# Banded attention in front of a mixture of experts: the row maxima leave the exponential, and copies change engines

## The chip, the cores and the metric

The kernel runs on one core of one Trainium2 chip. The metric is device time in microseconds (us) for one execution; smaller is better. Five engines of the core matter here, each with its own queue that is worked off in order: TensorE (PE; its weight loads are shown apart as PEld), VectorE (DVE), ScalarE (ACT), GpSimd (POOL) and SyncE (SP), which only issues DMAs here.

## The reference, cut to what matters

```python
scores = (1 / sqrt(64)) * q @ k.T            # batch 8, heads 8, sequence 576, head size 64
mask   = (rel >= 0) & (rel < 64)             # rel = row position - column position
scores = where(mask, scores, -1e9)
scores = scores - max(scores, axis=-1)       # row maximum
attn   = exp(scores)
attn   = attn / (sum(attn, axis=-1) + 1e-9)
x      = attn @ v                            # 4608 tokens x 512

logits = x @ w_gate                          # 8 experts, 576 tokens each at most
# (token, expert) pairs taken in descending order of logit; each token gets one expert
out[mask_e] = relu(x[mask_e] @ w1[e]) @ w2[e]
```

## The kernel before

**Three stages.** The attention comes first (to about 162 us in the profile), then the first pass of the routing, then the experts with the later routing passes between them. All instructions are put down in an order written by hand; each engine keeps that order, and waits only for the data or buffers of its next instruction. The change touches only the attention and the constants that the routing prepares while the attention runs.

**Attention.** A row block has 64 query rows, and needs the 128 keys that end with its own. Two blocks make 128 partitions; with `m` counting the pairs of blocks (36) and `g` the two halves of the eight heads, there are 72 units `(m, g)`, each of four heads. The loop over `s` (76 iterations) is a software pipeline over these units, and in iteration `s` it puts down:

- `qk` for unit `s`: 16 small score products on PE into `Sp` in PSUM (L126), then on DVE for each of the four heads one custom operation (L135) that adds the mask, scales, writes the negated scores `st`, and leaves the row minimum of them in a column of `mx` (a second, short instruction reads that accumulator). After each of the four, one small step of `norm` for unit `s-4` follows: `r` = row sum + 1e-9 (L203), its reciprocal (L204), the gate values (L188, and every eighth time a sum over heads, L192), the values `x` (L198).
- `sm` for unit `s-1`: four exponentials on ACT, one for each head, with the column of `mx` as bias (L145), giving `pe`.
- `tr` for unit `s-2`: four transposes on PE into the one PSUM buffer `Tp` (L152) and one copy of all four to `pt` on ACT (L154).
- `pv` for unit `s-3`: 16 products on PE with `pt` as weights and the values as moving data (L173). The last of the 73 columns of a value row is 1, so the row sum comes with it; columns 64 to 71 hold the gate products.
- whatever is put down for that iteration in a table `at`, one step of the routing's choices (`late`, six small DVE operations for every four pairs `m`), and one step of the routing's constants (`setup`, a generator; three steps in iterations 4 to 9).

**Values.** `VO[b]` holds a batch's value rows for odd blocks as loaded. `VE[b]` is the same moved by 64 partitions, for even blocks; `even` makes it with two 64x584 copies for each of its four slices `j` (L111, L112), on GpSimd, except the first two slices of batch 0, which are on VectorE. The gate columns are computed on the side, for each batch in two parts: `gate_mm` (PE, L85), `gate_cp` (ACT, L89) in one iteration, `gate_tr` (PE, L95), `gate_out` (DVE, L101 and L104, into columns 64 to 71 of `VO`) and `even` in the next. For batch 2 these iterations are 15 to 18, and then 24 to 27, 34 to 37, 43 to 46, 52 to 55 and 61 to 64. All four gate steps share one PSUM buffer `pvt`.

**Loads.** SP issues the loads of batch `b` in iteration 9(b-2)+5, in the order `VT`, `Q`, `K`, `VO`; a load waits until its buffer is free (two of `VT`, three of the others).

**Constants.** `constants` makes tables for the routing in 64 small steps, 61 of them on DVE (L386 to L437) and three on GpSimd (L401, L403).

Of the kernel before, what the change touches and what calls it, by code (L numbers as in the profile page):

```python
# [30 lines left out]
def attention(ctx, tc, c, q, k, v, vt, gate, xs, L, choices, setup, counters):  # L31
# [65 lines left out]
    def gate_out(b, i0, i1):  # L97
# [16 lines left out]
    PT_, PB, ST, OP_ = {}, {}, {}, {}  # L114

    def qk(m, g, old):
# [13 lines left out]
        st = wk.tile([128, 4, 128], FT, name="st")  # L130
        mx = wk.tile([128, 4], FT, name="mx")
        nrm = norm(*old) if old else []
        for h in range(4):
# [3 lines left out]
            if nrm:  # L137
                nrm.pop(0)()
        ST[m, g] = (st, mx)

    def sm(m, g):
        st, mx = ST.pop((m, g))
        pe = wk.tile([128, 4, 128], FT, name="pe")
        for h in range(4):
            nc.scalar.activation(pe[:, h, :], st[:, h, :], AF.Exp, bias=mx[:, h:h + 1], scale=-1.0)  # L145
        PB[m, g] = pe

    def tr(m, g):
        Tp = ps.tile([128, 4, 128], FT, name="Tp", bufs=1)
        pe = PB.pop((m, g))  # L150
# [26 lines left out]
    def norm(m, g):  # L177
# [52 lines left out]
    for b in range(B):  # L230
        s0 = 9 * (b - 1) + (6 if b < 4 else 7)
        for i, s in zip(PARTS, ((1, 5), (7, 11))[b] if b < 2 else (s0, s0 + 2)):
# [13 lines left out]

    for s in range(n + 4):
        old = seq[s - 4] if 4 <= s else None
        if s < n:
            qk(*seq[s], old)  # L250
        else:
            rs, inv, gates, values = norm(*old)

            for f in (rs, inv, values, gates) if s < n + 2 else (rs, inv, gates):
                f()
# [15 lines left out]
        if late:  # L271
            late.pop(0)()
        if s > 3:
            for _ in range(3 if s < 10 else 1):
# [794 lines left out]
```

## Time and profile before

| | us |
|---|---|
| median of 3 runs | 668.48 (667.67 to 670.57) |
| the profiled execution | 668.27 |
| its span, first to last instruction | 666.6 |
| PE busy | 634.8 (95%) |
| DVE busy | 444.3 (67%) |
| ACT busy | 363.2 (54%) |
| POOL busy | 187.8 (28%) |

The span is 1.67 us shorter than the execution's own time. Busy shares are averages over three stages with different limits; PE's end times are modelled, so a PE that is shown busy may be waiting for short times, and the distances between starts are the safer reading. In a row of the timeline the columns are the start in us, the duration in us, engine, line, operation, output<-input, shapes, count of merged instructions, and in square brackets how long the engine had been idle and what ended that.

### The profile page before, as it was taken

To read this page: it belongs to the slowest core of one execution; us is meant where nothing else is said; L and a number is where in the kernel's file an instruction comes from. 1 tells how busy PE (TensorE), PEld (TensorE's weight loads), DVE (VectorE), ACT (ScalarE), POOL (GpSimd) and SP (SyncE) were. 2 spreads that over 40 slices of the span, in tenths; PEclk is the share of its full clock that TensorE was granted. 3 is DMA by queue.
4 is the path that set the end of the run, shared out by engine and by line. 5 is a ranking of instruction groups with operands and counts; after the bars stand their busy time and mean duration, and the time that the engine had idled before them with its cause. 6 is when DMAs were issued, how large, how long until landed. Compare 5 with 4: busy or idle time off the path is not lost. (4 is left out here: it accounts for less than half of the span.)

```text
span 666.6 us, 16956 instructions
## 1 busy us (share of the span) xinstructions
PE 634.8 (95%) x6383; PEld 533.4 (80%) x6383; DVE 444.3 (67%) x2246; ACT 363.2 (54%) x734; POOL 187.8 (28%) x218
## 2 busy tenths in 40 slices
PE   7989999998579999999999999999999999999995
PEld 5667777776459878987997898789789879988984
DVE  5878898888777766885786688478668852303300
ACT  5778998886046247427624652762465276256310
POOL 0433233330052034206202420620252062042211
PEclk8999999999579999999999999999999999999999
DMA  9999988922068369829766982976698299939701
GB/s 302 342 370 372 372 324 311 390 79 74 10 205 212 67 215 237 182 58 289 200 118 228 220 191 58 287 196 117 228 212 186 60 294 270 234 99 222 143 25 47
DMA packets 50097, 134.10 MB, mean 201 GB/s; under 512 B 4696, under 2 KB 10968, under 8 KB 50016
## 3 DMA queue, kind: packets, MB, share of 16 engines
q0 software_dynamic: 15280, 52.98, 35.7%
q1 hardware_dynamic: 34192, 79.52, 33.4%
q8 instruction: 50, 0.82, 0.5%
q10 hardware_dynamic: 544, 0.52, 0.2%
q14 instruction: 31, 0.25, 0.1%
HBM read 82.15 MB, written 18.87 MB: 152 GB/s over the span
## 5 line engine op out<-in xcount | busy, mean ns | idle before, releaser
L949 POOL DMA_INDIRECT out<-ot,idx x40 | 41.6, 1041 | 299.2 <-DVE ab L629 100.9
L899 ACT ACTIVATE hh<-h 128x256 fp32r<-128x256 f32 (+1 forms) x128 | 52.2, 408 | 105.5 <-PE h L927 104.5
L969 PE MATMUL o<-wh,hl 128*128 128x512 f32 x256 | 102.8, 401 | 0.0
L969 PE MATMUL o<-wl,hh 128*128 128x512 f32 x256 | 101.8, 397 | 0.0
L969 PE MATMUL o<-wh,hh 128*128 128x512 f32 x256 | 101.5, 397 | 0.0
L927 PE MATMUL h<-xh,wl 128*128 128x256 f32 (+1 forms) x512 | 93.2, 299 | 0.0
L135 DVE CUSTOM_DVE_ANT_0 st<-Sp,mask 128x128 f32<-128x128 f32 x288 | 78.9, 278 | 20.8 <-PE Sp L126 14.1
L145 ACT ACTIVATE pe<-st,mx 128x128 f32<-128x128 f32 x288 | 91.2, 391 | 2.7 <-DVE mx L135 2.7
L927 PE MATMUL h<-xl,wh 128*128 128x256 f32 (+1 forms) x512 | 92.0, 298 | 0.4 <-DVE xl L860 0.4
L927 PE MATMUL h<-xh,wh 128*128 128x256 f32 (+1 forms) x512 | 90.9, 299 | 0.7 <-ACT xh L856 0.7
L904 DVE SCALAR_TENSOR_TENSOR hl<-h,hh 128x256 fp32r<-128x256 f32 x128 | 53.4, 417 | 56.7 <-ACT hh L899 55.7
L927 PEld LDWEIGHTS h<-xh,wh 128*128 128x128 f32 x512 | 75.5, 189 | 1.6 <-ACT xh L856 0.8
L927 PEld LDWEIGHTS h<-xh,wl 128*128 128x128 f32 x512 | 76.2, 189 | 0.2
L927 PEld LDWEIGHTS h<-xl,wh 128*128 128x128 f32 x512 | 75.5, 189 | 0.7 <-DVE xl L860 0.6
L811 ACT ACTIVATE wh<-st 128x1024 fp32r<-128x1024 f32 x64 | 67.2, 1050 | 6.7 <-DMA st<-w 6.7
L820 ACT ACTIVATE wl<-wh 128x1024 fp32r<-128x1024 f32 x61 | 64.4, 1056 | 0.9
L822 POOL DMA_DIRECT2D wl<-st x61 | 57.2, 1258 | 16.0 <-ACT wl L820 15.6
L969 PEld LDWEIGHTS o<-wl,hh 128*128 128x128 f32 x256 | 48.1, 188 | 9.0
L969 PEld LDWEIGHTS o<-wh,hl 128*128 128x128 f32 x256 | 48.3, 189 | 8.7
L969 PEld LDWEIGHTS o<-wh,hh 128*128 128x128 f32 x256 | 48.2, 188 | 8.5
L173 PE MATMUL Op<-VO,pt 128*64 128x73 f32 x640 | 52.4, 233 | 0.4 <-DVE x L198 0.3
L860 DVE TENSOR_TENSOR xl<-tp,xh 128x512 fp32r<-128x512 f32 (+1 forms) x40 | 25.3, 631 | 40.0 <-ACT xh L856 39.9
(178 smaller groups left out, 1117.0 us busy)
## 6 DMA issues: line engine op xcount, KB each, us to landing
wl<-st POOLq DMA_DIRECT2D x61, 512.0 KB
st<-w SPq DMA_DIRECT2D x60, 512.0 KB, 5.7
xs<-x SPq DMA_DIRECT2D x36, 256.0 KB, 5.3
VO<-v SPq DMA_DIRECT2D x6, 1168.0 KB
VT<-vt SPq DMA_DIRECT2D x6, 1152.0 KB, 8.9
Q<-q SPq DMA_DIRECT2D x6, 1152.0 KB
K<-k SPq DMA_DIRECT2D x6, 1152.0 KB, 16.4
VO<-v SPq DMA_DIRECT2D x4, 584.0 KB
```

Source lines behind the costliest of these rows:

```text
L135: nc.vector.tensor_tensor_reduce(st[:, h, :], Sp[h % 2][:, h // 2], mk, scale=-0.125, scalar=3.0e38, op0=OP.add, op1=OP.min, accum_out=mx[ ...
L145: nc.scalar.activation(pe[:, h, :], st[:, h, :], AF.Exp, bias=mx[:, h:h + 1], scale=-1.0)
L173: nc.tensor.matmul(Op[64 * a:64 * a + 64, h, :], pt[:, h, 64 * a:64 * a + 64], vv[a][:, 4 * g + h, :], start=True, stop=True)
L811: nc.scalar.activation(hi, st[i], AF.Copy)
L820: nc.scalar.activation(lo, hi.bitcast(FT), AF.Copy, scale=-1.0)
L822: nc.gpsimd.dma_start(lo.bitcast(FT), st[i], accum_op=OP.add)
L860: nc.vector.tensor_tensor(xl[:, :, r], t[:, :, :n], xh[:, :, r].bitcast(FT), OP.subtract)
L899: nc.scalar.activation(hh[:, f, c0:c1], h, AF.Relu)
L904: nc.vector.scalar_tensor_tensor(t, h[:, a - c0:b - c0], 0.0, hh[:, f, a:b].bitcast(FT), op0=OP.max, op1=OP.subtract)
L927: nc.tensor.matmul(h, wv[:, cc, 128 * (f % 2):128 * (f % 2) + 128], xt[:, cc, c0:c1], start=(k == 0), stop=(k == 11))
L949: nc.gpsimd.indirect_dma_start(out=self.out, out_offset=IndirectOffsetOnAxis(ap=idx[0:m, a:a + 1], axis=0), in_=ot[0:m], in_offset=None)
L969: nc.tensor.matmul(o, ht[:, f, 128 * a:128 * a + 128], wt[:, 512 * (f % 2):512 * (f % 2) + 512], start=(k == 0), stop=(k == 23))
```

## The change

- **Maxima.** `sm` becomes one GpSimd subtraction for all four heads, in place: `st` minus `mx`, the column spread over 128 elements. The transposes take `st`, and the copy after them becomes the exponential of all four heads at once. `st` and `mx` get four buffers instead of three.
- **Row sums.** `r` = sum + 1e-9 goes from DVE to ACT, and is put down at the head of iteration `s`, ahead of everything else of ACT.
- **Gate columns and even blocks.** `gate_out` goes from DVE to ACT. The even blocks go from GpSimd to ACT, but for the first two slices of batch 0, which stay on VectorE; slices 2 and 3 come two and four iterations later than before.
- **Order on VectorE.** Within `qk` the reciprocal and the gate values come after the second head, the values, the step of the choices and the steps of the constants after the third, and the fourth head is last.
- **Constants.** The shift table is made by one operation instead of eight, `gt` by one instead of five, `s5` by two instead of 32, with three more iotas on GpSimd at the start. 23 steps remain.

```diff
@@ gate_out, even
-        nc.vector.tensor_copy(VO[b][:, j0:j1, :, 64:72],
-                              pt[:, :128 * n].rearrange("p (j h g) -> p j h g", j=n, h=8)[:, :, :, :8])
+        nc.scalar.activation(VO[b][:, j0:j1, :, 64:72],
+                             pt[:, :128 * n].rearrange("p (j h g) -> p j h g", j=n, h=8)[:, :, :, :8], AF.Copy)
         if i1 % 2:
-            nc.vector.tensor_copy(VO[b][0:64, 4, :, 64:72],
-                                  pt[:64, 128 * n:128 * n + 128].rearrange("p (h g) -> p h g", h=8)[:, :, :8])
+            nc.scalar.activation(VO[b][0:64, 4, :, 64:72],
+                                 pt[:64, 128 * n:128 * n + 128].rearrange("p (h g) -> p h g", h=8)[:, :, :8], AF.Copy)
...
-    def even(b, j, eng):
-
-        eng.tensor_copy(VE[b][0:64, j], VO[b][64:128, j])
-        eng.tensor_copy(VE[b][64:128, j], VO[b][0:64, j + 1])
+    def even(b, j, early):
+
+        for d, e in ((slice(0, 64), j), (slice(64, 128), j + 1)):
+            a = VE[b][d, j], VO[b][64 - d.start:128 - d.start, e]
+            if early:
+                nc.vector.tensor_copy(*a)
+            else:
+                nc.scalar.activation(*a, AF.Copy)
@@ qk, sm, tr
-        st = wk.tile([128, 4, 128], FT, name="st")
-        mx = wk.tile([128, 4], FT, name="mx")
-        nrm = norm(*old) if old else []
+        st = wk.tile([128, 4, 128], FT, name="st", bufs=4)
+        mx = wk.tile([128, 4], FT, name="mx", bufs=4)
         for h in range(4):
 
             nc.vector.tensor_tensor_reduce(st[:, h, :], Sp[h % 2][:, h // 2], mk, scale=-0.125, scalar=3.0e38,
                                            op0=OP.add, op1=OP.min, accum_out=mx[:, h:h + 1])
-            if nrm:
-                nrm.pop(0)()
+            for f in (nrm[0:2], nrm[2:] + [small])[h - 1] if h in (1, 2) else ():
+                f()
...
-        st, mx = ST.pop((m, g))
-        pe = wk.tile([128, 4, 128], FT, name="pe")
-        for h in range(4):
-            nc.scalar.activation(pe[:, h, :], st[:, h, :], AF.Exp, bias=mx[:, h:h + 1], scale=-1.0)
-        PB[m, g] = pe
+        st, mx = ST[m, g]
+        nc.gpsimd.tensor_tensor(st, st, mx[:, :, None].to_broadcast([128, 4, 128]), OP.subtract)
...
-            nc.tensor.transpose(Tp[:, h, :], pe[:, h, :], c["ident"])
+            nc.tensor.transpose(Tp[:, h, :], st[:, h, :], c["ident"])
         pt = wk.tile([128, 4, 128], FT, name="pt")
-        nc.scalar.activation(pt, Tp, AF.Copy)
+        nc.scalar.activation(pt, Tp, AF.Exp, scale=-1.0)
@@ norm
-        return [lambda: nc.vector.tensor_scalar(r, Op[:, :, 72], 1e-9, None, op0=OP.add),
-                lambda: nc.vector.reciprocal(r, r), gates, values]
+        nc.scalar.activation(r, Op[:, :, 72], AF.Copy, bias=1e-9)
+        return [lambda: nc.vector.reciprocal(r, r), gates, values]
@@ the table at, and the loop over s
-                    put(s + 1, even, b, j, nc.gpsimd if b or j > 1 else nc.vector)
+                    put(s + 1 + 2 * max(0, j - 1), even, b, j, not b and j < 2)
...
+    def small(s):
+        if late:
+            late.pop(0)()
+        if s > 3:
+            for _ in range(3 if s < 10 else 1):
+                next(setup, None)
...
-            qk(*seq[s], old)
+            qk(*seq[s], norm(*old) if old else [], lambda: small(s))
         else:
-            rs, inv, gates, values = norm(*old)
-
-            for f in (rs, inv, values, gates) if s < n + 2 else (rs, inv, gates):
+            inv, gates, values = norm(*old)
+
+            for f in (inv, values, gates) if s < n + 2 else (inv, gates):
@@ constants (counters makes sh and v5 with three iotas)
-        for r in range(NR):
-            yield nc.vector.tensor_scalar(tab[:, r], dg, 28 - 4 * r, None, op0=OP.logical_shift_left)
+        yield nc.vector.tensor_tensor(tab, dg[:, None, :].to_broadcast([128, NR, ND]),
+                                      self.sh[:, :, None].to_broadcast([128, NR, ND]), OP.logical_shift_left)
...
-        for k in range(5):
-
-            yield nc.vector.tensor_scalar(gt[:, k:k + 1], jp[0:32, 8 * k:8 * k + 1], 0.0, None, op0=OP.is_le)
+        yield nc.vector.tensor_scalar(gt, jp[0:32, 0:33:8], 0.0, None, op0=OP.is_le)
...
+        w5 = t("w5", [72, 2, 4, 5])
+        yield nc.vector.tensor_scalar(w5, self.v5, 0.0, None, op0=OP.is_equal)
+        yield nc.vector.scalar_tensor_tensor(s5, self.v5, -36.0, w5, op0=OP.is_equal, op1=OP.add)
```

## Rows read from the trace of the kernel before

**Rows 1.** The page's busy time by engine, and the granted clock and DMA share in 40 slices of 16.7 us.
```profile
PE 634.8 (95%) x6383; PEld 533.4 (80%) x6383; DVE 444.3 (67%) x2246; ACT 363.2 (54%) x734; POOL 187.8 (28%) x218
...
PEclk8999999999579999999999999999999999999999
DMA  9999988922068369829766982976698299939701
```

**Rows 2.** The view of stretches, from iteration 18 to the last score product: length, then busy time and count of PE, PEld, DVE, ACT, POOL, the granted clock, DMA share, GB/s.
```profile
47.20:156.80 109.60, 109.18 (x2024) 80.05 (x2020) 95.68 (x749) 96.57 (x277) 31.61 (x48) 1.00 0.82 296
```

**Rows 3.** The timeline of PEld over one iteration without gate work (31): score products, transposes, the first value product, the next score products.
```profile
78.11 0.43 PEld L126 LDWEIGHTS Sp<-K,Q 64*64 64x64 f32 x16
78.71 0.42 PEld L152 LDWEIGHTS Tp<-ident,pe 128*128 128x128 f32 x4 [0.17 <-ACT pe L145]
79.30 0.13 PEld L173 LDWEIGHTS Op<-VO,pt 128*64 128x64 f32 x1 [0.17 <-DVE mx L135]
...
79.96 0.42 PEld L126 LDWEIGHTS Sp<-K,Q 64*64 64x64 f32 x16
```

**Rows 4.** The timeline of DVE over the same iteration: first and third head, the steps between them, the end, and the next iteration's first head.
```profile
78.94 0.29 DVE L135 CUSTOM_DVE_ANT_0 st<-Sp,mask 128x128 f32<-128x128 f32 x1 [0.18 <-PE Sp L126]
79.16 0.08 DVE L135 DVE_READ_ACCUMULATOR2_ANT mx<- 128x1 f32 x1
79.16 0.16 DVE L203 TENSOR_SCALAR r<-Op 128x4 f32<-128x4 f32 x1
79.23 0.28 DVE L135 CUSTOM_DVE_ANT_0 st<-Sp,mask 128x128 f32<-128x128 f32 x1
...
80.02 0.42 DVE L198 TENSOR_TENSOR x<-Op,r 128x256 f32<-128x256 f32 x1
80.36 0.15 DVE L426 TENSOR_SCALAR sx<-jp 72x4 f32<-72x4 int32 x1
80.79 0.29 DVE L135 CUSTOM_DVE_ANT_0 st<-Sp,mask 128x128 f32<-128x128 f32 x1 [0.28 <-PE Sp L126]
```

**Rows 5.** The groups of instructions by line and shape from 40 to 160 us, ACT and DVE: busy us, mean ns.
```profile
L145 ACT ACTIVATE pe<-st,mx 128x128 f32<-128x128 f32 x228 | 72.2, 391 | 0.0
...
L154 ACT ACTIVATE pt<-Tp 128x512 f32<-128x512 f32 x58 | 34.4, 593 | 6.7 <-PE Tp L152 3.8
...
L89 ACT ACTIVATE vs<-pvt 128x256 f32<-128x256 f32 x6 | 2.3, 384 | 3.6 <-PE pvt L85 3.6
```

**Rows 6.** The page's groups: a long copy on ACT.
```profile
L820 ACT ACTIVATE wl<-wh 128x1024 fp32r<-128x1024 f32 x61 | 64.4, 1056 | 0.9
```

**Rows 7.** The groups by line and shape of POOL up to 160 us.
```profile
L112 POOL COPY VE<-VO 64x584 f32<-64x584 f32 x30 | 20.3, 676 | 19.3 <-DVE VO L101 14.4 <-DVE VO L104 3.8
...
L401 POOL IOTA r<- 128x1152 bf16 x1 | 1.2, 1243 | 0.1
```

**Rows 8.** The timeline of ACT, a copy and the four exponentials behind it.
```profile
79.47 0.60 ACT L154 ACTIVATE pt<-Tp 128x512 f32<-128x512 f32 x1
79.96 1.27 ACT L145 ACTIVATE pe<-st,mx 128x128 f32<-128x128 f32 x4
```

**Rows 9.** The timeline of PEld around the gate work of batch 3 (iterations 27 to 30): transposes of the gate values, then score products and transposes.
```profile
68.25 0.28 PEld L95 LDWEIGHTS pvt<-ident,vs 128*128 128x128 f32 x3
68.73 0.42 PEld L126 LDWEIGHTS Sp<-K,Q 64*64 64x64 f32 x16 [0.20 <-issue]
69.33 0.42 PEld L152 LDWEIGHTS Tp<-ident,pe 128*128 128x128 f32 x4 [0.17 <-ACT pe L145]
...
71.17 0.42 PEld L152 LDWEIGHTS Tp<-ident,pe 128*128 128x128 f32 x4 [0.17 <-ACT pe L145]
...
73.17 0.42 PEld L152 LDWEIGHTS Tp<-ident,pe 128*128 128x128 f32 x4 [0.17 <-ACT pe L145]
```

**Rows 10.** The timeline of DVE and of PE about 46 us (batch 2's gate values, iterations 16 to 18), in this order: one row of DVE, three of PE.
```profile
46.23 0.29 DVE L101 COPY VO<-pvt 128x128 f32<-128x128 f32 x1 [2.96 <-DMA VO<-v]
...
46.57 0.74 PE L85 MATMUL pvt<-VT,wgs 128*32 128x320 f32 x8 [1.50 <-DVE VO L101]
...
47.84 0.66 PE L152 MATMUL Tp<-ident,pe 128*128 128x128 f32 x4
48.84 0.28 PE L173 MATMUL Op<-VO,pt 128*64 128x73 f32 x1 [0.34 <-DVE x L198]
```

**Rows 11.** The waits of PE up to 50 us, summed: what waited for what, us in total, times, longest.
```profile
PE Op L173 <- DVE VE L112: 1.1, 1, 1.1
```

**Rows 12.** The waits from 40 to 160 us: PE's weight loads for GpSimd.
```profile
PEld Op L173 <- POOL VE L112: 0.6, 3, 0.3
```

**Rows 13.** The timeline of DVE: the same comparison of the choices twice.
```profile
37.06 0.43 DVE L449 TENSOR_TENSOR oh<-L,m 128x32 bf16<-128x32 f32 x1
...
73.30 0.17 DVE L449 TENSOR_TENSOR oh<-L,m 128x32 bf16<-128x32 f32 x1
```

**Rows 14.** The timeline of POOL at the first of these.
```profile
36.78 0.67 POOL L112 COPY VE<-VO 64x584 f32<-64x584 f32 x1
```

**Rows 15.** The timeline at the end of the attention: on DVE the first head of the last score products, on PE the last transposes, on ACT the copy behind them, and on DVE the last row sum, its reciprocal, and the last step of the choices.
```profile
157.58 0.29 DVE L135 CUSTOM_DVE_ANT_0 st<-Sp,mask 128x128 f32<-128x128 f32 x1 [0.25 <-PE Sp L126]
...
160.43 0.66 PE L152 MATMUL Tp<-ident,pe 128*128 128x128 f32 x4 [0.36 <-ACT pt L154]
...
161.19 0.60 ACT L154 ACTIVATE pt<-Tp 128x512 f32<-128x512 f32 x1 [0.81 <-PE Tp L152]
...
162.62 0.16 DVE L203 TENSOR_SCALAR r<-Op 128x4 f32<-128x4 f32 x1 [0.21 <-PE Op L173]
162.81 0.18 DVE L204 RECIPROCAL r<-r 128x4 f32<-128x4 f32 x1
...
164.58 0.19 DVE L455 TENSOR_TENSOR one<-w,best 128x32 bf16<-128x32 bf16 x1
```

More of the change, by code (lines that the diff above doesn't have):

```diff
@@ L100, in gate_out, with qk @@
         n = j1 - j0
-        nc.vector.tensor_copy(VO[b][:, j0:j1, :, 64:72],
-                              pt[:, :128 * n].rearrange("p (j h g) -> p j h g", j=n, h=8)[:, :, :, :8])
+        nc.scalar.activation(VO[b][:, j0:j1, :, 64:72],
+                             pt[:, :128 * n].rearrange("p (j h g) -> p j h g", j=n, h=8)[:, :, :, :8], AF.Copy)
         if i1 % 2:
-            nc.vector.tensor_copy(VO[b][0:64, 4, :, 64:72],
-                                  pt[:64, 128 * n:128 * n + 128].rearrange("p (h g) -> p h g", h=8)[:, :, :8])
+            nc.scalar.activation(VO[b][0:64, 4, :, 64:72],
+                                 pt[:64, 128 * n:128 * n + 128].rearrange("p (h g) -> p h g", h=8)[:, :, :8], AF.Copy)
         if not i0:
             VE[b] = ld.tile([128, 4, H, VW], FT, name="VE")
-    def even(b, j, eng):
-        eng.tensor_copy(VE[b][0:64, j], VO[b][64:128, j])
-        eng.tensor_copy(VE[b][64:128, j], VO[b][0:64, j + 1])
-    PT_, PB, ST, OP_ = {}, {}, {}, {}
-    def qk(m, g, old):
+    def even(b, j, early):
[5 more added lines that the diff above has]
+                nc.scalar.activation(*a, AF.Copy)
+    PT_, ST, OP_ = {}, {}, {}
+    def qk(m, g, nrm, small):
         Sp = [t[g] for t in SP]
@@ L136, in qk @@
                                            op0=OP.add, op1=OP.min, accum_out=mx[:, h:h + 1])
-            if nrm:
-                nrm.pop(0)()
+            for f in (nrm[0:2], nrm[2:] + [small])[h - 1] if h in (1, 2) else ():
+                f()
         ST[m, g] = (st, mx)
     def sm(m, g):
-        st, mx = ST.pop((m, g))
-        pe = wk.tile([128, 4, 128], FT, name="pe")
-        for h in range(4):
-            nc.scalar.activation(pe[:, h, :], st[:, h, :], AF.Exp, bias=mx[:, h:h + 1], scale=-1.0)
-        PB[m, g] = pe
+        st, mx = ST[m, g]
+        nc.gpsimd.tensor_tensor(st, st, mx[:, :, None].to_broadcast([128, 4, 128]), OP.subtract)
     def tr(m, g):
         Tp = ps.tile([128, 4, 128], FT, name="Tp", bufs=1)
-        pe = PB.pop((m, g))
+        st, mx = ST.pop((m, g))
         for h in range(4):
-            nc.tensor.transpose(Tp[:, h, :], pe[:, h, :], c["ident"])
+            nc.tensor.transpose(Tp[:, h, :], st[:, h, :], c["ident"])
         pt = wk.tile([128, 4, 128], FT, name="pt")
-        nc.scalar.activation(pt, Tp, AF.Copy)
+        nc.scalar.activation(pt, Tp, AF.Exp, scale=-1.0)
         PT_[m, g] = pt
@@ L270, in attention @@
             f(*a)
-        if late:
+        if s >= n and late:
             late.pop(0)()
-        if s > 3:
-            for _ in range(3 if s < 10 else 1):
-                next(setup, None)
     for f in last:
@@ L368, in __init__ @@
         t("dg", [128, ND], I32)
+        t("sh", [128, NR], I32)
+        t("v5", [72, 2, 4, 5], I32)
         t("lane", [128, 1])
@@ L377, in counters @@
         iota(self.dg, pattern=[[1, ND]], base=1, channel_multiplier=0)
+        iota(self.sh, pattern=[[-4, NR]], base=28, channel_multiplier=0)
+        iota(self.v5, pattern=[[1, 2], [2, 4], [8, 5]], base=0, channel_multiplier=-1)
+        iota(self.v5[:, :, 2:4, 4], pattern=[[1, 2], [2, 2]], base=32, channel_multiplier=-1)
         iota(self.rows, pattern=[[0, 1]], base=0, channel_multiplier=1)
@@ L418, in constants @@
         s5 = t("s5", [72, 2, 4, 5], BF)
-        for h in range(2):
-            for g in range(4):
-                for k in range(2):
-                    n = 5 if g < 2 else 4
-                    o = 36 * k + 2 * g + h
-                    w = t(f"sx{k}", [72, 5])
-                    yield nc.vector.tensor_scalar(w[:, 0:n], jp[0:72, o:o + 8 * n - 7:8], 0.0, None, op0=OP.is_equal)
-                    if g > 1:
-                        yield nc.vector.tensor_scalar(w[:, 4:5], jp[0:72, o + 28:o + 29], 0.0, None, op0=OP.is_equal)
-                    if k:
-                        yield nc.vector.tensor_tensor(s5[:, h, g], w0, w, OP.add)
-                    w0 = w
+        w5 = t("w5", [72, 2, 4, 5])
+        yield nc.vector.tensor_scalar(w5, self.v5, 0.0, None, op0=OP.is_equal)
+        yield nc.vector.scalar_tensor_tensor(s5, self.v5, -36.0, w5, op0=OP.is_equal, op1=OP.add)
         t("st", [128, 5, E])
```

## The prediction

> **What bounds the kernel now.** I read the page first: PE is busy for 95% of the span, and no other engine comes near [rows 1]. That is an average over stages, so I cut the attention out with the view of stretches. From 47.2 us, where iteration 18 begins, to the last score product at 156.8 us, PE is busy 109.18 of 109.60 us, at a granted clock of 1.00 (the 2.4 GHz level), while DVE and ACT both stand at about 88% and POOL at 29% [rows 2]. "Busy" is modelled, so I checked it on the starts of one iteration without gate work: score products at 78.11, transposes at 78.71, value products at 79.30, next score products at 79.96, hence 0.60 + 0.59 + 0.66 = 1.85 us [rows 3]. The 0.17 us ahead of the transposes and of the value products is there with any releaser, so it belongs to PE's own work. DVE waits for PE once in each iteration (0.28 us at 80.79) [rows 4]. So in this stretch the three busy engines are near each other, but PE sets the pace, and the change takes nothing from PE: 16 score products, four transposes and 16 value products stay.
>
> Ahead of the stretch something else rules. At 46.23 DVE's copy of the gate columns of batch 2 had waited 2.96 us for the load of VO, and PE had stood 1.50 us behind it [rows 10]; the DMA engines are at 8 or 9 tenths in every slice up to 83 us [rows 1]. That load is last of three batches in a queue that is always full, and the change moves no load. Whatever the first 46 us gain is lost in this wait, and what they lose is hidden up to the same amount.
>
> **The change part by part.**
>
> *Work taken off DVE and ACT after 47 us: nothing gained.* DVE loses the row sum (0.07 us between starts, 79.16 to 79.23) [rows 4], the gate copies and 41 constant steps; ACT loses four exponentials of 0.391 us for one larger one. PE hides all of it. What can be won is what PE still lost: 109.60 − 109.18 = 0.42 us [rows 2], and of the waits for GpSimd's even blocks three times 0.6/3 − 0.17 = 0.03 us, 0.1 us in all [rows 3, 12]. I take 0.1.
>
> *The subtraction on GpSimd.* No row shows POOL with two inputs. The nearest is its copy of 584 columns, 0.676 us, that is 1.16 ns a column [rows 7]. Bounds for 512 columns: as fast as one input 0.59; three passes (two reads, one write) 1.78. Two inputs read one after the other give 1.19, and I take 1.2. The Trainium skill (GPSIMD Engine Reference, "Performance versus the Vector engine") measures 4497 ns for an addition of 2048 columns and advises against elementwise work there; a quarter is an estimated 1.12 us, which would leave the sum as it is; no run here shows it yet.
>
> Is it in time? Now the fourth head comes last. Counting from DVE's first head: values start at 80.02 − 78.94 = 1.08; without the row sum (0.07) and the fourth head (79.23 − 78.94 less 0.07, 0.22) 0.79; values 0.34 (80.36 − 80.02); a step of the choices up to 0.17 [rows 13]; fourth head 0.22 and its accumulator read 0.08: 1.60. DVE's first head is 0.83 behind PE's score products (78.94 − 78.11), a hand-over costs 0.10 (161.19 less 160.43 + 0.66) [rows 15], so the subtraction runs from 2.53 to 3.73 and PE may go on at 3.83. The transposes of that unit are due at 2 x 1.85 + 0.60 = 4.30. 0.47 us are left: up to 1.67 us the subtraction costs nothing. At 1.78 it would cost 0.1 in each iteration. Behind it on POOL stand only three iotas of the constants (1.24 us the longest [rows 7]), in iterations 6 and 7, ahead of 46 us.
>
> *Gate columns and even blocks on ACT.* ACT takes 0.384 for 256 columns [rows 5] and 1.056 for 1024 [rows 6]: 0.875 ns a column and 0.16 fixed; so 0.67 for an even copy, 0.27 and 0.22 for the two gate copies, 0.16 for a row sum, 0.391 + 384 x 0.875 ns = 0.73 for the new exponential. Two in a row overlap by 0.11 (79.47 + 0.60 against 79.96) [rows 8]. The queue of ACT in an iteration is now: row sum, exponential, gate copies, even copies. The tight place is the second gate iteration of a batch, followed by an iteration without gate work. In batch 3 the gate transposes start at 68.25 and end about 0.51 later (0.66 for four, less one of 0.15) [rows 9, 15]; gate copies from 68.86 (hand-over 0.10) to 69.24, even copies 69.24 to 70.47, row sum to 70.52, exponential 70.41 to 71.14. Behind this exponential waits the next set of transposes, since there is one Tp: released at 71.24, it started at 71.17 before [rows 9]. That is 0.07 late. The row sum at 70.52 holds DVE's reciprocal, and by it the rest of that iteration: 0.1 hand-over, reciprocal and gate values 0.2, third head 0.22, values 0.34, choices 0.17, fourth head 0.30 give 71.85; the subtraction ends at 73.15, and its transposes, at 73.17 before [rows 9], come at 73.25: no later than PE already is. Waits of ACT on its own writes aren't in any row; I take 0.15 a batch. Bounds: 0 (a little idle was there) and 0.7 (no overlap, 4 x 0.11, and two hand-overs more, with the subtraction late behind it). Batches 2 to 7: 6 x 0.15 = 0.9.
>
> *The wait at 46 us moves to ACT.* Behind the gate copy that waits for VO now stand two even copies, a row sum and the exponential: 46.23 + 0.27, + 2 x 0.67 − 0.11, row sum, exponential end at 48.40; Tp is free at 48.50 instead of 47.84, the value products come at 49.10 instead of 48.84 [rows 10]: 0.26.
>
> *Up to 46 us.* PE loses 1.1 us there for even copies on DVE [rows 11], and 1.50 in the wait: 2.6 us of cover. New costs: those two DVE copies beside a subtraction, 0.5 to 1.9; iteration 8, which has two slices for ACT (4 x 0.56, gate copy and exponential 0.8, against an iteration of 2.2), 0.9; iterations 10 and 12, 0.1 to 0.3. 1.5 to 3.1 against 2.6: I take 0, at the worst 0.5. Without that cover it would be the whole sum.
>
> *The end.* The last unit has no successor to hide behind. Its first head was at 157.58; + 1.60 + 0.10 + 1.2 + 0.10 = 160.58 for transposes that stood at 160.43 [rows 15]: 0.15. The exponential is 0.13 longer than the copy; the last row sum goes by ACT, one hand-over more, 0.1. Together 0.4, all in front of the last step of the choices at 164.58, on which the routing waits.
>
> Sum: −0.1 + 0.9 + 0.26 + 0 + 0.4 = 1.5 us. Against the profiled execution (span 666.6 and 1.67 around it, 668.27) that is 669.8; the median of the runs, 668.48, stands 0.2 above that execution, which I leave out. Routing and experts do the same work and only start later.
>
> **The rivals.** *GpSimd's port decides (slower).* A comparison of the choices took 0.43 us instead of 0.17, and ended with the GpSimd copy that ran beside it (37.49 and 37.45) [rows 13, 14]. Four of the six steps of the choices read two SBUF tensors like this one. They now stand between the third and the fourth head, while the subtraction of the unit before may still run, and the next subtraction waits for the fourth head: a loop of subtraction + 0.10 + 0.17 + 0.30. At 1.2 that is 1.77, under 1.85; it decides from 1.28 on. At 1.78 it is 2.35, 0.50 too much in four iterations of eight, seven such groups after 47 us: 14 us, 682. For it: DVE is at 88%. Against: in most iterations the step comes 1.14 + 0.25 us behind the last fourth head, when a subtraction of 1.2 is over.
> The Trainium skill has this rule (SBUF — State Buffer, "SBUF: two separate sides"): DVE operations with two SBUF inputs or in a two-port mode and GpSimd exclude each other for whole instructions; the trace agrees, with the 0.43 above.
>
> *ACT's queue costs more (slower).* At the upper bound, 6 x 0.7 + 0.7 at 46 us + 0.4 = 5.3 us: 673.6. For it: ACT carries 1.12 us of even copies in front of the next exponential. Against: five of nine iterations have no even copies at all, and there they stand behind the exponential.
>
> *PE's last losses go (faster).* If ACT's queue is always in time, the gain is at most 0.42 us [rows 2] and the 0.36 idle at 160.43 [rows 15]: 667.5. That is also the case in which the change does what it says and nobody waits for it.
>
> **How the numbers follow.** About 0.5% (3.3 us) is what a measurement of this kernel can tell from no change: 665.0 to 671.6. My sum (668.5 to 671.6) 0.48; PE's last losses go 0.17; ACT's queue, 671.6 to 674, 0.18; GpSimd's port, 674 to 682, 0.12; something that I don't see and that gains over 3.3 us, 0.05, since a gain after 46 us has no place on PE. So faster 0.05, same 0.65, slower 0.30. The range from 667.0 to 677 leaves out the 0.05, a little of the small gain, and the larger half of the port's case.
>
> **What would show it.** The subtraction's mean near 1.2 us; starts of the score products still 1.85 apart without gate work; PE again waiting for the gate copy (now ACT) at 46.2; after each second gate iteration a transposition that waits for ACT by some tenths; DVE's idle time grown, for PE; the last step of the choices near 166. The prediction is wrong if PE's starts after 47 us are further apart in iterations without gate work (the port), or if VO of batch 2 lands earlier.

## The result, and the profile after

The changed kernel took 673.82 us (median of 5 runs, 671.36 to 674.58); the kernel before, beside it, 668.0. The ratio is 1.0072 (95% interval 1.0053 to 1.009): slower by about 5 us (the ratio is that of the means; the medians are 5.8 us apart). The profiled execution took 673.82 us, with a span of 672.2.

The page's busy time by engine, of the kernel after:
```profile
PE 636.1 (95%) x6383; PEld 533.8 (79%) x6383; DVE 439.1 (65%) x2109; ACT 334.0 (50%) x602; POOL 221.4 (33%) x233
```
The view of stretches, kernel after, from iteration 18 to the last score products (columns as in [rows 2]):
```profile
48.20:162.30 114.10, 110.12 (x2022) 79.96 (x2018) 90.64 (x634) 76.91 (x183) 55.06 (x53) 1.00 0.78 282
```
ACT and DVE got lighter, and GpSimd, which took work over, still has room: ACT is busy for 76.91 us here and for 96.57 before, DVE for 90.64 and 95.68 [rows 2]. Yet the stretch is 4.5 us longer (0.77 of it is a pause of this one execution, experiment 11), and PE, which did the same work, is now idle for 114.10 − 110.12 = 3.98 us of it, against 0.42. Less work on ACT, and PE waits: shares of busy time can't show that, the waits can.

The view of waits, kernel after, 47 to 165 us (us in total, times, longest):
```profile
DVE r L204 <- ACT r L203: 12.4, 20, 1.9
...
PEld Tp L152 <- POOL st L146: 3.0, 9, 0.6
PEld Op L173 <- DVE x L198: 2.5, 8, 0.7
PE Tp L152 <- ACT r L203: 1.8, 7, 0.5
PE Op L173 <- DVE x L198: 1.0, 3, 0.4
```
The first row isn't on PE and would cost nothing by itself. It is the root of the third and fifth, as "The row sum" below shows. The fourth names the row sum, which was the last thing to end; by the code the exponential ahead of it holds `Tp`.

Where PE lost it is read best from the starts of the score products, iteration by iteration. (Counted from the start, the iteration at 78.11 in [rows 3], called 31 there, is 33 when the first is 0, as everywhere else; nothing hangs on it.) A "step to 21", or a loss "at 21", is the distance from the start of iteration 20 to that of 21, so the wait lies in iteration 20. I compare a second execution of each kernel (the runs `before_again` and `after_again` below):

| stretch (iterations) | PE's loss, us | what it waits for |
|---|---|---|
| 0 to 10 | 0.45 | 0.36 at 8, for two even copies on DVE (0.14 against the first profile of before) |
| 11 to 17 | 1.92 | ACT: two slices of even blocks in iteration 8, then one at a time |
| 18 | −1.57 | the wait for VO, which absorbs this |
| 19 to 22 | 1.14 | 0.14 at 19: ACT, two slices in iteration 16; 0.75 at 21: exponential late 0.26, row sum late 0.49; 0.24 at 22: subtraction late |
| 23 to 33 | 0.23 | ACT, batch 3 (the kernel before itself loses 0.14 at 30) |
| 34 to 51 | 0.70 | ACT, batches 4 and 5 |
| 52 to 60 | 0.74 | 0.38 at 53: row sum late; 0.36 at 58 and 59: ACT |
| 61 to 70 | 0.95 | 0.26 at 67: ACT; 0.31 at 69: row sum late; 0.13 at 62 and 0.24 at 70: subtraction late |
| behind them, to the last step of the choices | 0.19 | last unit |

The sum is 4.75 us: the last step of the choices stands at 169.79 instead of 165.04. What follows differs by 1.1 to 1.4 us between two executions of one kernel (502.02 and 503.46 us for the kernel before, 501.87 and 503.01 after), so the 4.3 us between the two spans agree with it.

**A batch, seen on ACT.** ACT, kernel after, second gate iteration of batch 4 and what follows:
```profile
92.74 0.29 ACT L101 ACTIVATE VO<-pvt 128x128 f32<-128x128 f32 x1 [0.55 <-PE pvt L95]
92.92 0.21 ACT L104 ACTIVATE VO<-pvt 64x64 f32<-64x64 f32 x1
93.14 1.40 ACT L116 ACTIVATE VE<-VO 64x584 f32<-64x584 f32 x2
94.57 0.17 ACT L203 ACTIVATE r<-Op 128x4 f32<-128x4 f32 x1
94.64 0.59 ACT L154 ACTIVATE pt<-Tp 128x512 f32<-128x512 f32 x1
```
PEld at the same time:
```profile
94.48 0.43 PEld L130 LDWEIGHTS Sp<-K,Q 64*64 64x64 f32 x16
95.34 0.42 PEld L152 LDWEIGHTS Tp<-ident,st 128*128 128x128 f32 x4 [0.44 <-issue]
...
96.59 0.42 PEld L130 LDWEIGHTS Sp<-K,Q 64*64 64x64 f32 x16
97.29 0.42 PEld L152 LDWEIGHTS Tp<-ident,st 128*128 128x128 f32 x4 [0.27 <-POOL st L146]
```
From the gate copy to the end of the exponential ACT needs 95.23 − 92.74 = 2.49 us. The transposes were due 0.60 behind the score products, at 95.08, and come at 95.34: 0.26 late. One iteration on they are due at 97.19 and come at 97.29, now behind the subtraction: 0.10 more. Together 0.36 in this batch.

**The double slice.** ACT, kernel after, iterations 8 and 9:
```profile
26.63 1.39 ACT L116 ACTIVATE VE<-VO 64x584 f32<-64x584 f32 x2
28.05 0.29 ACT L101 ACTIVATE VO<-pvt 128x128 f32<-128x128 f32 x1
28.37 1.39 ACT L116 ACTIVATE VE<-VO 64x584 f32<-64x584 f32 x2
29.78 0.17 ACT L203 ACTIVATE r<-Op 128x4 f32<-128x4 f32 x1
29.85 0.59 ACT L154 ACTIVATE pt<-Tp 128x512 f32<-128x512 f32 x1
```
PE, the transposes behind that exponential:
```profile
30.59 0.63 PE L152 MATMUL Tp<-ident,st 128*128 128x128 f32 x4 [1.18 <-ACT r L203]
```
**The row sum.** DVE, kernel after, while PE is in iteration 20 (reciprocal, gate values, sum over heads, then values):
```profile
53.31 0.18 DVE L204 RECIPROCAL r<-r 128x4 f32<-128x4 f32 x1 [0.80 <-ACT r L203]
53.52 0.19 DVE L188 TENSOR_TENSOR l<-Op,r 128x32 f32<-128x32 f32 x1
53.75 0.62 DVE L192 TENSOR_REDUCE L<-l 128x32 f32<-128x256 f32 x1
...
54.49 0.42 DVE L198 TENSOR_TENSOR x<-Op,r 128x256 f32<-128x256 f32 x1
```
PEld at the same time, the transposes and the first value product, which needs the buffer `Op` that the values free:
```profile
53.88 0.42 PEld L152 LDWEIGHTS Tp<-ident,st 128*128 128x128 f32 x4 [0.43 <-issue]
54.96 0.13 PEld L173 LDWEIGHTS Op<-VO,pt 128*64 128x64 f32 x1 [0.67 <-DVE x L198]
```
The row sum stood behind two even copies on ACT. DVE had waited 0.80 us for it, every eighth unit sums over heads too (0.62 us), and the values came so late that PE stood. The step from iteration 20 to 21 is 2.61 us after, 1.86 before. With the 0.17 that is always there taken off, 0.26 of the difference is the late exponential, as in batch 4, and about 0.5 the late values.

**A third way.** In iterations that sum over heads, the third and fourth head now stand behind that sum, and so the subtraction does. PEld, kernel after, two iterations on:
```profile
141.50 0.42 PEld L152 LDWEIGHTS Tp<-ident,st 128*128 128x128 f32 x4 [0.30 <-POOL st L146]
```
0.17 of this is there with any releaser [rows 3]; 0.13 is a loss. It returns at 62 in every kernel here with the new order on DVE, and at 70 in all but run 3 below. At 22 and 70 the changed kernel loses 0.24, where the row sum is late as well; with single copies (run 2 below) it is 0.15 and 0.12.

### The profile page after: what moved, and what is told of

The parts are those of the page before. It is cut to its first block, busy times and chain, and to the rows that moved or that the text cites. A ratio compares the mean times of both kernels' runs of the same rounds, so it can differ in the third digit from the quotient of the medians.

```text
span 672.2 us, 16833 instructions
## 1 busy us (share of the span) xinstructions
PE 636.1 (95%) x6383; PEld 533.8 (79%) x6383; DVE 439.1 (65%) x2109; ACT 334.0 (50%) x602; POOL 221.4 (33%) x233
## 5 line engine op out<-in xcount | busy, mean ns | idle before, releaser
L146 POOL TENSOR_TENSOR st<-st,mx 128x512 f32<-128x512 f32 x72 | 75.1, 1042 | 86.2 <-DVE mx L138 70.4
L138 DVE CUSTOM_DVE_ANT_0 st<-Sp,mask 128x128 f32<-128x128 f32 x288 | 73.9, 286 | 17.2 <-PE Sp L130 16.3
L154 ACT ACTIVATE pt<-Tp 128x512 f32<-128x512 f32 x72 | 42.9, 596 | 39.0 <-PE Tp L152 39.0
L965 PEld LDWEIGHTS o<-wh,hh 128*128 128x128 f32 x256 | 48.2, 188 | 8.6
```

Source lines behind the costliest of these rows:

```text
L138: nc.vector.tensor_tensor_reduce(st[:, h, :], Sp[h % 2][:, h // 2], mk, scale=-0.125, scalar=3.0e38, op0=OP.add, op1=OP.min, accum_out=mx[ ...
L146: nc.gpsimd.tensor_tensor(st, st, mx[:, :, None].to_broadcast([128, 4, 128]), OP.subtract)
L154: nc.scalar.activation(pt, Tp, AF.Exp, scale=-1.0)
L965: nc.tensor.matmul(o, ht[:, f, 128 * a:128 * a + 128], wt[:, 512 * (f % 2):512 * (f % 2) + 512], start=(k == 0), stop=(k == 23))
```

## The experiments

Theory: TensorE loses its time to ScalarE's queue, where two even copies of 0.69 us in a row stand in front of a row sum and an exponential. Rivals: the row sum by itself; GpSimd's subtraction or its port; something of the execution and not of the change. Iterations are counted as in the table; run 3 is experiment 3, and so on.

**1. `rsum_dve`: the row sum back on DVE.**
```diff
-        nc.scalar.activation(r, Op[:, :, 72], AF.Copy, bias=1e-9)
-        return [lambda: nc.vector.reciprocal(r, r), gates, values]
+        def inv():
+            nc.vector.tensor_scalar(r, Op[:, :, 72], 1e-9, None, op0=OP.add)
+            nc.vector.reciprocal(r, r)
+        return [inv, gates, values]
```


> Theory: the changed kernel (673.8 us, +5.8 against before) loses its time where ACT's two even copies (1.39 us together) stand in front of the next row sum and the next exponential. DVE waits for row sums for 12.4 us after 47 us, and by that the values and the release of the two Op buffers come late; where the sum over heads (0.62 us) falls into the same iteration, PE waits (0.76 us in iteration 20, 0.38 in 52, 0.54 in 68 and 69). With the row sum back on DVE these three places go, the 0.25 us per batch of the late exponential stay: 671.5 to 672.5 us, and no wait of DVE for a row sum. Rival 1, only the exponential's delay matters: the same three places stay, 673.5 or more. Rival 2, GpSimd's subtraction or its port is what is late: no change, 673.8.

Measured: 672.15 us, 1.0055 (1.0039 to 1.0072). As expected: the step at 21 falls from +0.75 to +0.19, which is the exponential's, the one at 53 from +0.38 to +0.07, and the late exponentials stay. The row sum is a part of the loss, about 1.7 us by the medians, not all of it. The two intervals overlap, so it is the steps that show it: from iteration 18 to the last this profile loses 1.2 us less than that of `after_again`, 1.8 without its pause of 0.63 at 33 (see 11).

**2. `even_split`: the two copies of a slice in successive iterations.**
```diff
-    def even(b, j, early):
...
-        for d, e in ((slice(0, 64), j), (slice(64, 128), j + 1)):
+    def even(b, j, early, part=(0, 1)):
...
+        for d, e in [((slice(0, 64), j), (slice(64, 128), j + 1))[i] for i in part]:
...
-                    put(s + 1 + 2 * max(0, j - 1), even, b, j, not b and j < 2)
+                    if not b and j < 2:
+                        put(s + 1, even, b, j, True)
+                        continue
+                    for k_ in range(2):
+                        put(s + 1 + k_ + 2 * max(0, j - 1) - (not b), even, b, j, False, (k_,))
```
The last slices of batch 0 also come one iteration earlier.

> The same even copies on ACT, but the two of a slice in two successive iterations (one copy an iteration; those of batch 0 one iteration earlier). Theory (the two copies in one go hold up row sum and exponential): the chain in front of them is 0.70 us shorter, so the 0.35 us a batch, the losses at the sums over heads and most of the double slices in iterations 8 and 16 go: 669 to 670.5 us, with PE's starts of score products 1.85 us apart in nearly all iterations without gate work. Rival 1, ACT's total load or a count of its instructions matters: 673 to 674. Rival 2, the subtraction or the port of GpSimd: 673.8.

Measured: 668.58 us, 1.0005 (0.9992 to 1.0017): level with the kernel before, better than expected. ACT, the same place in batch 4:
```profile
90.40 0.29 ACT L101 ACTIVATE VO<-pvt 128x128 f32<-128x128 f32 x1 [0.55 <-PE pvt L95]
90.58 0.21 ACT L104 ACTIVATE VO<-pvt 64x64 f32<-64x64 f32 x1
90.80 0.69 ACT L116 ACTIVATE VE<-VO 64x584 f32<-64x584 f32 x1
91.39 0.15 ACT L203 ACTIVATE r<-Op 128x4 f32<-128x4 f32 x1
91.58 0.60 ACT L154 ACTIVATE pt<-Tp 128x512 f32<-128x512 f32 x1
92.21 0.69 ACT L116 ACTIVATE VE<-VO 64x584 f32<-64x584 f32 x1
```
The view of waits, 47 to 165 us:
```profile
DVE r L204 <- ACT r L203: 2.9, 4, 1.6
...
PEld Op L173 <- DVE x L198: 0.7, 4, 0.2
```
The same work on the same engine, with one copy behind the exponential instead of two in front of it. The steps at 11, 21, 40, 49, 53, 58 and 67 are gone, most of the wait for the row sum with them; 0.15 at 22, 0.13 at 62 and 0.12 at 70 stay.

**3. `even_pool`: the even blocks back on GpSimd at the times of before, all else as changed.**
```diff
-    def even(b, j, early):
...
-                nc.scalar.activation(*a, AF.Copy)
+    def even(b, j, eng):
...
+        eng.tensor_copy(VE[b][0:64, j], VO[b][64:128, j])
+        eng.tensor_copy(VE[b][64:128, j], VO[b][0:64, j + 1])
...
-                    put(s + 1 + 2 * max(0, j - 1), even, b, j, not b and j < 2)
+                    put(s + 1, even, b, j, nc.gpsimd if b or j > 1 else nc.vector)
```


> The even copies back on GpSimd in the iterations of before, all else as changed. Theory: ACT is free, so the losses at ACT go (minus 3 to 4 us), but two copies of 0.67 us stand in front of a subtraction of 1.04 in four of nine iterations, 2.4 against 1.85 us, which uses up the 0.6 us of slack and gives back 0.2 to 0.5 us a batch: 670.5 to 673. If the subtraction and GpSimd's port were what is late in the changed kernel (rival), more work there makes it worse: 675 to 680.

Measured: 695.57 us, 1.0412 (1.039 to 1.0433): a miss, all theories far too low. POOL in the second gate iteration of a batch:
```profile
98.53 1.04 POOL L142 TENSOR_TENSOR st<-st,mx 128x512 f32<-128x512 f32 x1 [0.43 <-DVE mx L134]
99.64 0.67 POOL L111 COPY VE<-VO 64x584 f32<-64x584 f32 x1
...
103.21 0.67 POOL L112 COPY VE<-VO 64x584 f32<-64x584 f32 x1
103.96 3.03 POOL L142 TENSOR_TENSOR st<-st,mx 128x512 f32<-128x512 f32 x3
```
PEld, the transposes that wait for that subtraction:
```profile
105.05 0.72 PEld L148 LDWEIGHTS Tp<-ident,st 128*128 128x128 f32 x4 [2.89 <-POOL st L142]
```
Six copies in a row, 4.2 us, stand in front of the next subtraction. In the kernel before nothing urgent stood behind them: the 48 instructions of POOL in [rows 2] are the even copies. The wait isn't all: PE was busy for 0.67 us of the 3.26 up to 105.0, and from 105.0 to 108.4 the granted clock is 0.50 (1.2 GHz) instead of 1.00. So these transposes are 0.72 long and not 0.42, and from them to the next score products it is 2.22 us instead of 1.25. A batch loses about 4.2 us where the clock falls, and 2.7 in batch 6, where after the same wait it doesn't.

**4. `before_v_first`: the kernel before, with VO loaded ahead of Q and K.**
```diff
         load_vt(b, *ALL)
-        load_qk(b, *ALL)
         load_v(b, *ALL)
+        load_qk(b, *ALL)
```


> The kernel before, with the value loads of batches 2 to 7 put ahead of Q and K in SP's queue. Theory: the wait of 1.50 us at 46 us is for a load that stands last in a full queue and fixes the time up to there; with it ahead of Q and K the gate copy goes on at once, and the next thing that the queue fixes is K of batch 2 for iteration 18, which began at 47.24 and could begin at 45.7 but must wait for K until about 46.3: 0.9 us faster, 667.1 (0.5 to 1.5 us). Rival: the wait only moves (Q and K land as late as VO did, or other batches' loads become late): no change, 668.0 within 0.4.

Measured: 666.84 us, 0.9981 (0.9968 to 0.9993). As expected. The gate copy no longer waits for VO:
```profile
43.85 0.29 DVE L101 COPY VO<-pvt 128x128 f32<-128x128 f32 x1
```
The step to iteration 18 is 3.72 us instead of 4.09, to 19 2.36 instead of 2.74, so the wait of [rows 10] cost the kernel before 0.75 us by these steps. This profile loses 0.65 us in the first four iterations and 0.24 at 33, and by the last score product is level with the first profile of before; the gain rests on the times of the runs.

**5. `split_rsum`: 1 and 2 together.**

> Both remedies at once: the two even copies of a slice in successive iterations, and the row sum back on VectorE. Theory (the row sum cost only because it stood behind the pair of copies on ScalarE; with single copies it is nearly in time): what is left to win is the 2.9 us of summed waits of VectorE for the row sum in the run with single copies, of which most is hidden by TensorE; 668.0 to 668.6, against 668.58 with single copies alone. Rival (the two costs are independent and add): another 1.7 us, the gain of the row sum alone, 666.9.

Measured: 669.37 us, 1.0028 (1.0015 to 1.0041), slower than single copies alone. Neither theory. With single copies the row sum is hardly late on ACT, and on DVE it makes the values later again: small steps of 0.06 to 0.13 come about in and behind the iterations that sum over heads (21, 22, 53, 61, 62, 69, 70), 0.6 us in all. From iteration 18 to the last this profile loses 1.0 us more than that of run 2; the other 0.4 is a longer pause of PE at 78 us (below). The remaining difference of the medians isn't accounted for.

**6. `split_rsum_v`: 5, with the load order of 4.**

> As the run before, and the values VO loaded ahead of Q and K in each batch. Theory (the wait for VO of batch 2 at 46 us is a separate cost which both the kernel before and the changed one carry): the 1.4 us that this order gave the kernel before come off here too, 666.4 to 667.2. Rival (the changed kernel spends that wait as cover for its own losses up to 46 us, so that the earlier load only uncovers them): 667.8 to 668.6.

Measured: 668.0 us, 1.0003 (0.9986 to 1.0019): 1.4 us under the run before it, the theory's difference, but outside its range and inside the rival's. The steps to 18 and 19 are 3.52 and 2.35 us against 3.58 and 2.76, so the profiles show 0.5 us for the load order; another 0.82 is the pause at 33, which this execution doesn't have. Neither side is shown.

**7. `split_longer`: 2, with half of the subtraction done once more.**
```diff
+        junk = wk.tile([128, 2, 128], FT, name="junk")
+        nc.gpsimd.tensor_tensor(junk, st[:, 0:2], mx[:, 0:2, None].to_broadcast([128, 2, 128]), OP.subtract)
         nc.gpsimd.tensor_tensor(st, st, mx[:, :, None].to_broadcast([128, 4, 128]), OP.subtract)
```


> Single copies, and GpSimd's subtraction made longer: half of it (two heads) is done once more into a tile that nobody reads, about 0.52 us on top of 1.04. Theory (the subtraction has 0.47 us of slack up to 1.67 us in an iteration, and GpSimd's port is not what decides): no change against 668.58 to within 1 us, starts of the score products 1.85 apart without gate work. Rival (GpSimd's port with the steps of the choices; a loop of subtraction + 0.10 + 0.17 + 0.30, which decides from 1.28 us on): 1.56 + 0.57 = 2.13 against 1.85, 0.28 too much in four of eight iterations, some 28 iterations after 47 us: 7.8 us, 676.

Measured: 670.28 us, 1.004 (1.0028 to 1.0052). The extra piece took more than expected. POOL's groups up to 170 us:
```profile
L148 POOL TENSOR_TENSOR st<-st,mx 128x512 f32<-128x512 f32 x72 | 75.1, 1043 | 33.3 <-DVE mx L138 24.4 <-PE Sp L130 5.2 <-PE Tp L154 2.2
L147 POOL TENSOR_TENSOR junk<-st,mx 128x256 f32<-128x256 f32 x72 | 44.4, 617 | 7.9 <-DVE mx L138 7.3 <-DVE r L206 0.4
```
So 1.04 + 0.62 = 1.66 us, the edge of the slack of 1.67. PE loses 0.2 us each at 23, 24, 25, 33 and 71, waiting for the subtraction; by the last score products it is 0.60 us behind run 2 (whose profile has a pause of 0.42 at 33), and 0.7 more in the last unit, which nothing hides. More than the theory's 1 us, but the rival's loop would have cost 28 iterations 0.38 us each, over 10. That rival falls. Why just these iterations are late isn't shown.

**8. `pool_split`: single copies, on GpSimd.** The diff of 2, and `nc.gpsimd.tensor_copy(*a)` for the copy on ScalarE.

> Single copies of the even blocks, one in an iteration, on GpSimd instead of ScalarE (the first two slices of batch 0 on VectorE as before), behind the subtraction of that iteration. Theory (what cost 27 us with the even blocks on GpSimd was six copies of 0.7 us in a row in front of a subtraction, not the engine): 1.04 + 0.71 = 1.75 us of GpSimd in an iteration of 1.85, so it fits; 668.5 to 670. Rival (GpSimd can't carry both, because the subtraction must start when the fourth score maximum is there and finds the copy running, or its port holds up VectorE): 0.2 to 0.6 us in each of the six iterations of a batch with a copy, six batches, 676 to 690.

Measured: 669.3 us, 1.0023 (1.0012 to 1.0034). POOL, one batch:
```profile
92.77 1.04 POOL L146 TENSOR_TENSOR st<-st,mx 128x512 f32<-128x512 f32 x1 [0.43 <-PE Sp L130]
93.87 0.67 POOL L116 COPY VE<-VO 64x584 f32<-64x584 f32 x1
94.62 1.04 POOL L146 TENSOR_TENSOR st<-st,mx 128x512 f32<-128x512 f32 x1
95.72 0.66 POOL L116 COPY VE<-VO 64x584 f32<-64x584 f32 x1
```
Both fit, as the theory has it. Of the 27 us of run 3 some 1.5 are left once the six copies are taken apart; the engine wasn't the cause.

**9. `maxima_alone`: the kernel before, with the subtraction and the one exponential alone.** The diff is that of `sm` and `tr` above, with four buffers for `st` and `mx`.

> The kernel before with the subtraction on GpSimd and the one exponential alone (st and mx with four buffers); even blocks on GpSimd, gate columns, row sums, order and constants as before. Theory (six even copies of 0.7 us stand in a row in front of a subtraction in the second gate iteration of each batch, so that the core of the change can't be had without moving them): as the run with the even blocks back on GpSimd, 690 to 697. Rival (that loss came from the steps now on ScalarE or from the order on VectorE, which aren't in this kernel): 668 to 672.

Measured: 706.81 us, 1.0584 (1.0555 to 1.0613): the theory's direction, 10 us beyond its range. The six copies are the cause again:
```profile
111.50 1.12 PE L149 MATMUL Tp<-ident,st 128*128 128x128 f32 x4 [2.68 <-POOL st L143]
```
These transposes take 1.12 us instead of 0.66: with this wait the granted clock falls to 0.50 in each of the batches 2 to 7, for 3.4 us, in batch 4 for 6.8. Its mean from 47 to 190 us is 0.91. With the fall of 3.4 us a batch loses 4.2 us, as in run 3, and batch 4 loses 5.6. By the last score products this profile is 12.1 us behind that of run 3. Of these, 4.9 us are there by iteration 18, with the clock low in two stretches (32.6 to 36.0 and 46.2 to 49.6 us); the clock adds 1.4 us in batch 4 and 1.5 in batch 6; and the iteration ahead of the wait loses 0.6 to 0.9 us in five batches, where a subtraction stands behind two even copies and PE waits for it.

**10 and 11. `before_again` and `after_again`: both kernels once more, unchanged.**

> The kernel before, unchanged, profiled once more. Theory (two losses seen in several profiles, a later rise of the clock at 12 us, about 1 us, and a pause of TensorE inside the score products at 79 us, 0.2 to 0.8 us, belong to the execution and not to the kernel): one of them, or both, may show here too, and the time is 668 with either. Rival (the changed program brings them): starts of the score products at 13.6 and 78.1 us as in the first profile, with no such step.

> The changed kernel, unchanged, profiled once more and timed in more runs. Theory (of the 5.5 us by the last score product, 1.22 at iteration 11, 0.96 left at iteration 18, 0.99 in iterations 19 to 22 and 0.35 in each of four later batches are ScalarE's queue, and repeat; the 0.78 at iteration 33 is a pause of TensorE of that execution): the same steps at 11, 19, 21, 40, 49, 53, 58 and 67 to within 0.05 us, the one at 33 different; 672.3 to 673.8, ratio 1.006 to 1.009. Rival (the step at 33 belongs to the changed program): again 2.6 instead of 1.85.

Measured: 668.42 us, 1.0001 (0.9988 to 1.0013), and 673.77 us, 1.0078 (1.0054 to 1.0102). The changed kernel's steps repeat to 0.01 us at 11 (3.07), 12 (2.85), 21, 40, 49, 53, 58, 67, 69 and 70, to 0.08 at 19. The one at 33 does not. PE, first profile of the kernel after:
```profile
78.69 0.66 PE L130 MATMUL Sp<-K,Q 64*64 64x128 f32 x15
79.86 0.27 PE L130 MATMUL Sp<-K,Q 64*64 64x128 f32 x1 [0.52 <-issue]
```
PE, second profile of it:
```profile
80.76 0.67 PE L130 MATMUL Sp<-K,Q 64*64 64x128 f32 x16
81.36 0.33 PE L152 MATMUL Tp<-ident,st 128*128 128x128 f32 x1
```
The pause between the 15th and the 16th product makes the step 0.77 us longer. It is of the execution: the same program runs without it. The kernel before shows no such pause in either profile, so that part of the theory wasn't seen. Its first score products start 0.43 us apart in its two profiles, and the step to 4 is 1.85 and 2.14 us, with the granted clock at 1.00 from 11.6 us in one and from 12.8 in the other.

**12. `split_v`: 2, with the load order of 4.**

> Single even copies on ScalarE, row sum on ScalarE as changed, and VO loaded ahead of Q and K. Theory (the earlier load is worth 1.0 to 1.4 us for any of these kernels, and single copies cost 0.4 against the kernel before): 666.8 to 667.6, ratio 0.998 to 1.000, at best level with the kernel before with the same load order (0.9981). Rival (with TensorE the bound, what the attention gains at 46 us is taken back by the load of Q or K, which now lands later): 668.2 to 669.5.

Measured: 667.92 us, 0.9995 (0.9979 to 1.001). This is in neither range. The attention is over 0.79 us earlier than in the first profile of before (last step of the choices at 163.79), the time is level with it. Run 4 stays the only version whose interval lies below the kernel before, and it has nothing of the change.

## Why the prediction was right or wrong

The forecast was 669.8 us; 673.82 lies in the range of 667.0 to 677.0 and outside 665.0 to 671.6, which had 0.65. What happened is the rival "ACT's queue costs more" (671.6 to 674, 0.18), by another working than the one it was given: its 673.6 came from 0.7 us a batch and 0.7 at 46 us, where 0.24 to 0.36 and 0.14 to 0.22 were measured, and the rest of the measured loss came from places that had no term there. That the time lies in the range is in part luck; the sum was more than 3 us short.

- **PE as the bound: right.** Iterations that ACT and POOL don't hold up are 1.85 us apart at full clock in every kernel here, and where ACT's queue was mended (run 2), the lighter DVE and ACT still gained nothing: 668.58 against 668.21 beside it.
- **The subtraction: right in the main.** Taken 1.2 us, measured 1.04, in time except where a late row sum or a sum over heads puts off the fourth head (below); run 7 shows that the slack is about what was worked out, and that GpSimd's port isn't what decides here.
- **The step that failed: "I take 0.15 a batch".** The place was right, the second gate iteration of a batch with `Tp` released late. Its terms were off: two even copies take 1.40 us, start to next start 1.43, where 1.23 was taken with an overlap borrowed from a copy and exponentials of another shape [rows 8]; so the exponential starts 0.35 later behind the gate copy than worked out; it takes 0.59 instead of 0.73. That makes 0.26 instead of 0.07. "No later than PE already is" fell too: the subtraction came 0.10 late. 0.24 to 0.36 a batch instead of 0.15, 0.9 us more on the six batches.
- **A term that was missing.** I followed the late row sum to the subtraction, by way of DVE's queue, but not to the value products, by way of `Op`. In iterations that sum over heads, the values come 0.62 us later still, and PE stands: 0.49 of the 0.75 at 21, 0.38 at 53, 0.31 at 69, 1.2 us; run 1, which also takes the row sum out of the way of the exponential and the subtraction, puts its share at 1.7. The same sum over heads, which is not in my chain of 1.60 us to the subtraction, makes that late: 0.24 at 22, 0.13 at 62 and 0.24 at 70.
- **"Up to 46 us: I take 0": wrong, 0.80.** The losses there were 2.37 us, inside the 1.5 to 3.1 worked out. The cover was not 2.6: PE's 1.1 us for even copies on DVE [rows 11] was counted as cover, although those two copies stay on DVE in the change, and it waited 1.4 us for them after. What was left, 1.57, was absorbed. Iteration 8 was named with 0.9 and cost 1.22 (at 11); iterations 10 and 12, named with 0.1 to 0.3, cost 0.33 (at 12) and 0.37 (at 15 and 16).
- **The wait that moves to ACT: near in size, 0.14 to 0.22 against 0.26** at 19, by another working. ACT, kernel after:
```profile
45.44 1.39 ACT L116 ACTIVATE VE<-VO 64x584 f32<-64x584 f32 x2
46.93 0.29 ACT L101 ACTIVATE VO<-pvt 128x128 f32<-128x128 f32 x1
```
The gate copy came behind batch 1's last even copies, and PE no longer waited for it (the step to 18 is 2.53 us, no longer than the one to 27); the sign "PE again waiting for the gate copy" didn't come.
- **The end:** 0.19 against 0.4.

With the measured terms the prediction's own sum would have been 0.80 up to iteration 18, 0.14 at 19, 0.26 + 0.24 + 0.36 + 0.34 + 0.36 + 0.26 for batches 2 to 7, 1.18 for the late row sum, 0.61 for the subtraction behind sums over heads and 0.19 for the end: 4.74 of the 4.75 us.

## What to carry to other kernels

Work that is taken off an engine which isn't the bound pays nothing, and moving it can cost: what matters is not how full the new engine is but what stands right behind the moved instruction in its queue. So price the longest piece in a row against the slack of the first thing behind it, cut it (two copies of 0.69 us in two iterations left the time at 1.0005 of before, in one iteration at 1.0072), and follow each late result to every buffer it frees. A wait covers a loss in front of it only if that loss doesn't put off what ends the wait: the load of VO wasn't put off, and 1.57 us went under; the even copies on DVE moved along, and PE waited for them again.

## What the runs showed of the hardware

- Two copies of 64x584 on ACT from SBUF to SBUF don't overlap: 1.39 to 1.40 us, each 0.69. The first gate copy and the row sum beside them do overlap with what follows (92.74 + 0.29 against 92.92; 94.57 + 0.17 against 94.64). The Trainium skill (ScalarE: Activation LUTs, "What ACT_TABLE_LOAD costs") says that ACTIVATEs in a row overlap by about 93 ns; the trace agrees for the second kind and not for the first, and no run here says why.
- ACT's groups up to 170 us, kernel after: the exponential with one scale for 512 columns costs what the copy of before cost [rows 5].
```profile
L154 ACT ACTIVATE pt<-Tp 128x512 f32<-128x512 f32 x72 | 42.9, 596 | 39.0 <-PE Tp L152 39.0
L116 ACT ACTIVATE VE<-VO 64x584 f32<-64x584 f32 x60 | 41.3, 689 | 1.1
```
- POOL's subtraction with a column spread over 128 elements, kernel after: 1.04 us for 512 columns, less than the 1.2 taken from a copy; half of it takes 0.62 (run 7).
```profile
L146 POOL TENSOR_TENSOR st<-st,mx 128x512 f32<-128x512 f32 x72 | 75.1, 1042 | 86.2 <-DVE mx L138 70.4 <-PE Sp L130 8.1 <-PE Tp L152 6.4
```
- PE paused inside the score products of iteration 32, at 77 to 80 us, with the row put down to "issue", in five profiles of eleven of kernels with the change or its core (idle for 0.16 to 0.56 us by that row, the step 0.42 to 0.82 us longer), in neither of the kernel before. With the other load order (run 4) that kernel lost 0.24 us at the same place, inside the value products at 77.5 us. It wasn't there in the second profile of the changed kernel; whether the changed program makes it likelier, and what it waits for, stays open.
- PE's clock fell behind long waits (runs 3 and 9): after PE had stood for about 2.7 us before the transposes, the granted clock went from 1.00 to 0.50 for 3.4 us, once for 6.8, and transposes at that level took 1.12 us instead of 0.66. In batch 6 of run 3 the same wait was followed by no fall. In the changed kernel, where PE waits for another engine for 0.7 us at most from 48.2 to 162.3 us, it stayed at 1.00 there.
